# Folds behind the first stage as groups of products on halves of the array's rows, numerators in one piece, and two more steps before the transposes of an x tile

## The chip, the cores and the metric

The kernel runs on one core of one Trainium2 chip. The metric is the device time of one execution in microseconds (us), the median of several runs. The engines are named as the profile names them: PE (TensorE matmul), PEld (its weight load), DVE (VectorE), ACT (ScalarE), POOL (GpSimd) and SP (SyncE, which here issues every transfer between the core's memory and device memory, one after the other).

## The reference

The input x is 2048 x 1024 in float32. Its rows are normalised to xn. Two branches read xn, and the output is their combination:

```python
xn = _layernorm(x, axis=-1)
s = _A_ref(xn, A_wqkv, A_w_phi, A_wo)
g = _silu(_B_ref(xn, B_w_gate, B_w_up, B_w_down))
return x + s * g
```

Branch A is linear attention with 32 heads of width 32 and a learned feature map; branch B is a gated unit of inner width 3584.

```python
qkv = (lambda x, *d: x.transpose(*d))((x @ wqkv).reshape(B, S, 3, H, Dh), 2, 0, 3, 1, 4)
q, k, v = qkv[0], qkv[1], qkv[2]
pq = jnp.einsum("bhsd,hdf->bhsf", q, w_phi)
pk = jnp.einsum("bhsd,hdf->bhsf", k, w_phi)
phi_q = jnp.concatenate([_softmax(pq, axis=-1), _softmax(-pq, axis=-1)], axis=-1)
phi_k = jnp.concatenate([_softmax(pk, axis=-1), _softmax(-pk, axis=-1)], axis=-1)
kv = jnp.einsum("bhsf,bhsd->bhfd", phi_k, v)
num = jnp.einsum("bhqf,bhfd->bhqd", phi_q, kv)
...
# branch B
h = _sigmoid(g) * u
return jnp.einsum("bsf,fd->bsd", h, w_down)
```

Since pq is linear in q, the kernel multiplies w_phi into the q and k columns of wqkv first. That product is what the kernel calls a **fold**.

## The kernel before, in words

All large products are 128 x 128 by 128 x 512. Each operand is kept as a high and a low part, and `mm3` (lines 224 to 226) issues three products for one: high by high, high by low, low by high. Each large matrix product is cut into 2 x 2 blocks and computed with seven block products instead of eight; their names are B11, B21, T2, T3, T4, T1 and B22, in this order. For the projections, one such operation works on four token tiles u = 0..3, whose sums lie in the PSUM banks bank0 to bank3 (98 to 101 in the rows below); an operation is 4 x 4 `mm3`, 48 products. `proj_out` (line 497) takes each of the four sums from its bank behind the operation (`evac`, line 506, on DVE), and some of these results are stored to `qkv_d` at once (line 503). The two buffers for the stored results of T4 are used in turn, so that the third result waits for the first store, and the fourth for the second.

**The first stage** (normalisation, transposes, the first five operations of V for the first half of the tokens, and the folds K 0 to K 2) is written out as a table of steps, FIRST (line 95), and each engine keeps its order. The products stand there as line 996. The table ends with the four takings of T4's sums, in this order: "evac T4 3, ssub t1 1, wsub T1 0, evac T4 1, evac T4 2, evac T4 0".

**Behind it** the order is set by a scheduler, which puts instructions of several traced pieces together by its own estimate of the time; an instruction traced inside `tc.issue_after(i)` is not put ahead of instruction i, and instructions outside it move freely where their operands allow. The operations left of the first token half (V T1, V B22, then seven each for K and Q) are issued in the loop over `ops`; after each token tile's four `mm3`, `step()` takes one entry from the list `side`. The five folds K 3 and Q 0 to Q 3 are entries of that list. `fold(which, k)` loads four raw pieces (`fold_load`, line 323, from `wqkT`), multiplies each by the block-diagonal `bd` in four products of 128 x 128 by 128 columns (`fold_products`, line 329, "a quad" below), copies the results on ACT (`fold_copy`), forms sums on DVE and POOL (`fold_sum`, line 79) and stores seven blocks to `wf_d` (`fold_keep`, line 350), from which the later operations load their weights (line 469). Each record of the profile of such a product in float32 is a half of it, so a quad is 8 records and a fold 32. The raw pieces rotate through four half slots (slots 43 and 54), so a piece of the next fold is loaded when the products on the one before it are done.

**x tiles.** While Q and then the second half's operations run, `paced` spreads background tasks over the products. `x_task` (line 658) loads one tile of the second token half, normalises it, stores it to `xs_d`, loads it back in another arrangement (line 671), yields three times, and then transposes it on DVE (line 672) and forms the operands, with `x_sums` on POOL for every second tile. A yield is the point at which the task gives way until its next turn. The task counts for 8 turns in the pacing.

**The last stage** takes two token tiles at a time (eight pairs). For a pair, seven operations of 4 `mm3` run from the attention output against `wo`. Ahead of them lie the transposes of phi and `numerators` (line 822): 16 products with 64 output rows each (line 832), two of them next to each other in the array's columns, into bank0 to bank3.

The profile's line 220 and 219 are `split` (high part on ACT, low part on DVE), 917 and 920 the same in the first stage, and 1171 and 1188 take sums of the gated unit from their banks.

## Time and profile before

| | |
|---|---|
| time, median of 3 runs | 2351.0 us (2350.98 to 2352.16) |
| the profiled execution | 2350.23 us |
| its span, first to last instruction | 2348.5 us |
| mean granted TensorE clock | 0.999 |
| PE busy | 2331.4 us (99%), 10644 records |
| DVE / ACT / POOL busy | 1624.6 / 957.5 / 1160.7 us |
| transfers | 624.11 MB, mean 266 GB/s |

The profile page lists busy time by engine, the span in 40 slices, the transfer queue, the chain of work that ended last, and the costliest groups of instructions. A row of a group gives line, engine, operation, output and input names, shapes, the count, busy time, the mean of one instruction in ns, and the idle time of its engine just before, with what ended it. A busy PE is not PE at its peak: where products follow each other, the records overlap, so a product's cost is the distance between starts and not its duration.

### The profile page before, as it was taken

The page shows a single profiled execution, that of the slowest core. Times are in us where ns is not written, and L with a number is a line of the kernel's source. Part 1 is how long each engine was busy: PE and PEld are TensorE (multiplying, and loading weights), DVE is VectorE, ACT ScalarE, POOL GpSimd, SP SyncE. Part 2 cuts the span into 40 slices and gives each one's busy share as a digit, 9 for nine tenths or more (in the row PEclk, how much of TensorE's full clock was granted, in tenths as well). Part 3 has the DMA queues.
Part 4 walks back from the last instruction along what each step waited for, and adds up shares of the span by engine and source line. Part 5 has one row for each costly group of instructions (what it writes and reads, how often), then busy time and mean ns, then how long its engine had stood idle before and what let it go on. Part 6 is the DMA issues. An engine that isn't in the chain of part 4 may idle for free.

```text
span 2348.5 us, 32142 instructions
## 1 busy us (share of the span) xinstructions
PE 2331.4 (99%) x10644; PEld 1922.2 (82%) x10644; DVE 1624.6 (69%) x2306; ACT 957.5 (41%) x1410; POOL 1160.7 (49%) x1320
## 2 busy tenths in 40 slices
PE   9999999999999999999999999999999999999999
PEld 7888888878888888888888888888888888887777
DVE  8734788677777675466867777866666777657655
ACT  7333354445454454233435344433434333344322
POOL 3210267677686642304363544555444455623777
PEclk9999999999999999999999999999999999999999
DMA  8875566888888889858888887879777877878774
GB/s 289 298 266 188 188 213 223 278 291 300 304 309 294 281 300 362 303 186 281 270 274 284 281 270 262 287 249 344 245 235 258 276 240 232 285 261 296 241 226 162
DMA packets 265415, 624.11 MB, mean 266 GB/s; under 512 B 36896, under 2 KB 65696, under 8 KB 260640
## 3 DMA queue, kind: packets, MB, share of 16 engines
q1 hardware_dynamic: 265248, 622.05, 78.0%
q8 instruction: 84, 1.38, 0.2%
q14 instruction: 83, 0.68, 0.1%
HBM read 373.42 MB, written 248.51 MB: 265 GB/s over the span
## 4 chain that ended last, share of the span: by engine, by line
PE 90%; DMA 4%; DVE 4%; issue 1%; ACT 1%; POOL 0%; SPq 0%; DVEq 0%; ACTq 0%
PE bank L224 29%; PE bank L225 29%; PE bank L226 29%; DMA fa<-w_down 2%; PE bank L602 1%; PE bank L832 1%; PE bank L329 1%; DMA x<-xk 1%; DVE x L920 1%; DMA fc<-xs_d 0%; DVE x L220 0%; DVE w L220 0%; DMA fa<-wv 0%; DVE w L920 0%; DMA wf_d<-x 0%
## 5 line engine op out<-in xcount | busy, mean ns | idle before, releaser
L225 PE MATMUL bank<-x,w 128*128 128x512 f32 x2352 | 916.4, 390 | 0.7 <-DVE x L220 0.7
L224 PE MATMUL bank<-x,w 128*128 128x512 f32 x2352 | 906.3, 390 | 3.7 <-DVE fc L1171 2.1
L226 PE MATMUL bank<-x,w 128*128 128x512 f32 x2352 | 905.9, 389 | 0.0
L79 POOL TENSOR_TENSOR fc<-fc 128x256 f32<-128x256 f32 x488 | 427.4, 907 | 480.0 <-DMA fc<-e_d 131.6
L220 DVE TENSOR_TENSOR w<-fa,w 128x512 fp32r<-128x512 f32 (+1 forms) x436 | 397.6, 915 | 201.3 <-ACT w L219 191.6
L219 ACT CAST w<-fa 128x512 fp32r<-128x512 f32 (+1 forms) x436 | 300.3, 691 | 556.8 <-PE bank L225 354.5
L224 PEld LDWEIGHTS bank<-x,w 128*128 128x128 f32 x2352 | 441.9, 188 | 97.1 <-DVE fc L1171 2.7
L225 PEld LDWEIGHTS bank<-x,w 128*128 128x128 f32 x2352 | 442.0, 188 | 92.7 <-DVE x L220 1.9
L226 PEld LDWEIGHTS bank<-x,w 128*128 128x128 f32 x2352 | 441.8, 188 | 91.8
L224 PE MATMUL bank<-w,x 128*128 128x512 f32 x636 | 248.4, 391 | 0.3 <-DVE fc L506 0.3
L225 PE MATMUL bank<-w,x 128*128 128x512 f32 x636 | 247.9, 390 | 0.0
L226 PE MATMUL bank<-w,x 128*128 128x512 f32 x636 | 247.4, 389 | 0.0
L79 POOL TENSOR_TENSOR fb<-fa 128x256 f32<-128x256 f32 x112 | 97.9, 894 | 218.6 <-PE bank L226 110.9
L79 POOL TENSOR_TENSOR fb<-fb,fc 128x256 f32<-128x256 f32 x132 | 123.6, 957 | 121.8 <-DVE fc L1188 121.6
L79 POOL TENSOR_TENSOR fc<-fc,sa 128x256 f32<-128x256 f32 x128 | 97.0, 788 | 93.5 <-issue 85.0
L224 PEld LDWEIGHTS bank<-w,x 128*128 128x128 f32 x636 | 119.4, 188 | 26.9 <-issue 1.9
L226 PEld LDWEIGHTS bank<-w,x 128*128 128x128 f32 x636 | 119.4, 188 | 24.8
L225 PEld LDWEIGHTS bank<-w,x 128*128 128x128 f32 x636 | 119.4, 188 | 24.3
L219 ACT CAST p<-fc 128x512 fp32r<-128x512 f32 x96 | 73.0, 764 | 131.2 <-DVE fc L575 79.0
L220 DVE TENSOR_TENSOR x<-fa,x 128x512 fp32r<-128x512 f32 x112 | 93.9, 839 | 45.0 <-ACT x L219 45.0
L219 ACT CAST w<-fb 128x512 fp32r<-128x512 f32 x112 | 69.0, 617 | 118.2 <-PE bank L225 86.4
L1188 DVE TENSOR_TENSOR fc<-fc,bank 128x512 f32<-128x512 f32 x84 | 57.5, 684 | 83.5 <-PE bank L226 61.6
(208 smaller groups left out, 2824.3 us busy)
## 6 DMA issues: line engine op xcount, KB each, us to landing
ws_d<-w SPq DMA_DIRECT2D x112, 512.0 KB, 4.2
w<-ws_d SPq DMA_DIRECT2D x112, 512.0 KB, 5.2
fa<-w_gu SPq DMA_DIRECT2D x84, 512.0 KB, 4.8
fa<-h_d SPq DMA_DIRECT2D x84, 512.0 KB, 4.9
fa<-wf_d SPq DMA_DIRECT2D x32, 1024.0 KB, 6.1
h_d<-fc SPq DMA_DIRECT2D x120, 256.0 KB, 4.7
fa<-w_down SPq DMA_DIRECT2D x80, 256.0 KB, 5.2
h_d<-fb SPq DMA_DIRECT2D x76, 256.0 KB, 4.5
```

The lines of the kernel that those rows point to most:

```text
L79: last = self.engine.tensor_tensor(o[:, s], a[:, s], b[:, s], op=op)
L219: nc.scalar.copy(o[0], src)
L220: return nc.vector.tensor_sub(o[1], src, o[0].bitcast(F32))
L224: nc.tensor.matmul(o, a[0], b[0], start=first, stop=False, **kw)
L225: nc.tensor.matmul(o, a[0], b[1], start=False, stop=False, **kw)
L226: nc.tensor.matmul(o, a[1], b[0], start=False, stop=last, **kw)
L329: nc.tensor.matmul(ps[:, gs], r[:, gs], bd[:, 4 * (n // 2) + g], start=True, stop=True)
L602: nc.tensor.matmul(kvb[g // 2][:, g % 2 * 256:g % 2 * 256 + 256], v[:, g].rearrange("p a f -> p (a f)"), ph[:, g].rearrange("p a f -> p (a ...
L832: nc.tensor.matmul(ps[bs, j * 256:(j + 1) * 256], kv[:, 2 * j + b, bs], ph[:, 2 * j + b], start=True, stop=True, skip_group_check=True)
L920: nc.vector.tensor_sub(o[1], src, o[0].bitcast(F32))
L1188: v = nc.vector.tensor_add(b, u2 if q == 3 else u1, bank)
```

## The change

It has four parts.

1. The five folds behind the first stage are issued by a new function, `fold_group`: 32 products on 64 rows each in place of 16 on 128. `bd` holds 32 x 32 blocks on its diagonal, so the upper 64 rows of a raw piece only reach 64 of the 128 columns and the lower 64 rows the other 64; each half of the rows is multiplied by its 64 columns, and the two halves write two different banks. All 32 stand one after the other, behind the last `mm3` issued (`last_mm`), and the next `mm3` of the projection comes behind them. Four copies on ACT per fold remain, each now of one half of two pieces. Empty entries in `side` put two, one, two, two and two steps ahead of the five folds. The loads for K 3 are issued right behind the first stage, and the loads for the next fold inside each fold, now for Q 0 too.
2. All `mm3` of the projections of the first token half, and those of the last stage, stand behind the one issued before: their order is the order in which they are written, so token tile 0 (bank0) comes first in each operation.
3. The 16 products of `numerators` stand together behind the last `mm3`.
4. `x_task` yields five times ahead of the transposes in place of three, and counts for 10 turns in place of 8.

```diff
--- before.py
+++ after.py
@@ -36,6 +36,9 @@
 
     def next(self):
         self.n += 1
+        return self.now()
+
+    def now(self):
         return self.items[(self.n - 1) % len(self.items)]
 
 
@@ -223,7 +226,7 @@
 
         nc.tensor.matmul(o, a[0], b[0], start=first, stop=False, **kw)
         nc.tensor.matmul(o, a[0], b[1], start=False, stop=False, **kw)
-        nc.tensor.matmul(o, a[1], b[0], start=False, stop=last, **kw)
+        return nc.tensor.matmul(o, a[1], b[0], start=False, stop=last, **kw)
 
     def cut(ab, s):
         return ab[0][:, s], ab[1][:, s]
@@ -316,7 +319,7 @@
     fraw = Ring(halves(43, 11))
     fblock = {K: Ring(((4, 5), (6, 7), (52, 53), (50, 51))), Q: Ring(((52, 53), (50, 51)))}
 
-    folds, folded = {}, {}
+    folds, folded, last_mm = {}, {}, []
 
     def fold_load(which, k, n, r=None):
         r = folds[which, k, n] = fraw.next() if r is None else r
@@ -338,6 +341,38 @@
         else:
             nc.scalar.copy(b, ps)
 
+    def fold_group(which, k):
+
+        with tc.issue_after(last_mm[0]):
+            for n in range(4):
+                if n % 2 == 0:
+                    ps = [tps.next() for _ in range(2)]
+                r = folds.pop((which, k, n))
+                for g in range(4):
+                    for half in range(2):
+                        rs = slice(64 * half, 64 * half + 64)
+                        o = ps[half][:, n % 2 * 256:n % 2 * 256 + 256]
+                        if which == Q:
+                            o = o.rearrange("p (a g d) -> p g a d", a=2, d=DH)[:, g]
+                        else:
+                            o = o.rearrange("p (g f) -> p g f", g=4)[:, g]
+                        m = nc.tensor.matmul(o, r[rs, g * P:(g + 1) * P], bd[rs, 4 * (n // 2) + g, rs], start=True, stop=True,
+                                             skip_group_check=True)
+                if n % 2:
+                    fold_out(which, k, n // 2, ps)
+        last_mm[:] = [m.ins]
+
+    def fold_out(which, k, m, ps):
+        if (which, k) not in folded:
+            folded[which, k] = halves(*fblock[which].now())
+        b = whole(fblock[which].now()[m])
+        for half in range(2):
+            if which == Q:
+                o, l = b.rearrange("p (n g h d) -> p h n g d", n=4, h=2, d=DH)[:, half], ps[half].rearrange("p (n g d) -> p n g d", n=4, d=DH)
+            else:
+                o, l = b.rearrange("p (n h f) -> p h n f", h=2, f=64)[:, half], ps[half].rearrange("p (n f) -> p n f", f=64)
+            nc.scalar.copy(o, l)
+
     def fold_sum(which, k, i, engine):
         a11, a12, a21, a22 = folded[which, k]
         o, a, b, op = ((a22, a21, a22, ALU.add), (a21, a11, a21, ALU.subtract),
@@ -354,12 +389,12 @@
         for n in range(4):
             if (which, k, n) not in folds:
                 fold_load(which, k, n)
-        for n in range(4):
-            fold_copy(which, k, n, fold_products(which, k, n, tps.next()))
+        fblock[which].next()
+        fold_group(which, k)
         fold_keep(which, k, False)
-        if k < 3:
+        if (which, k) != (Q, 3):
             for n in range(4):
-                fold_load(which, k + 1, n)
+                fold_load(*((which, k + 1) if k < 3 else (Q, 0)), n)
         for i in range(4):
             fold_sum(which, k, i, (vector, pool)[i % 2])
         with tc.issue_after(last_sp[0]):
@@ -665,9 +700,8 @@
             nc.sync.dma_start(xs_d[t - CTT, :, :, n].rearrange("q s c -> s q c"),
                               xt[n * DH:(n + 1) * DH].rearrange("s (q c) -> s q c", q=4))
         nc.sync.dma_start(xt, xs_d[t - CTT].rearrange("q s n c -> (q s) (n c)"))
-        yield
-        yield
-        yield
+        for _ in range(5):
+            yield
         for q in range(2):
             nc.vector.transpose(dst[q].rearrange("p (k n s) -> p n k s", n=4, s=DH),
                                 xt.rearrange("p (n k d) -> p n k d", n=4, d=DH)[:, :, 4 * q:4 * q + 4])
@@ -822,16 +856,18 @@
     def numerators(tp_):
 
         sums = []
-        for hb in range(2):
-            for q in range(2):
-                ps, ph = nmr.next(), units_ph[hb, q]
-                kv = slots[KVB[hb]][:, q].rearrange("p (k m) -> p k m", m=P)
-                for j in range(2):
-                    for b in range(2):
-                        bs = slice(b * 64, b * 64 + 64)
-                        nc.tensor.matmul(ps[bs, j * 256:(j + 1) * 256], kv[:, 2 * j + b, bs], ph[:, 2 * j + b], start=True,
-                                         stop=True, skip_group_check=True)
-                sums.append((hb, q, ps))
+        with tc.issue_after(last_mm[0]):
+            for hb in range(2):
+                for q in range(2):
+                    ps, ph = nmr.next(), units_ph[hb, q]
+                    kv = slots[KVB[hb]][:, q].rearrange("p (k m) -> p k m", m=P)
+                    for j in range(2):
+                        for b in range(2):
+                            bs = slice(b * 64, b * 64 + 64)
+                            m = nc.tensor.matmul(ps[bs, j * 256:(j + 1) * 256], kv[:, 2 * j + b, bs], ph[:, 2 * j + b],
+                                                 start=True, stop=True, skip_group_check=True)
+                    sums.append((hb, q, ps))
+        last_mm[:] = [m.ins]
         for hb, q, ps in sums:
             o = oraw[hb].rearrange("p u (g t) -> p u g t", t=P)
             nc.scalar.copy(o[:, :, 2 * q:2 * q + 2], ps.rearrange("p (j u t) -> p u j t", j=2, u=2))
@@ -1044,8 +1080,11 @@
     fraw.items = halves(43, 54)
     while prep():
         pass
-    for w, k in [(K, 3)] + [(Q, k) for k in range(4)]:
+    for w, k, waits in ((K, 3, 2), (Q, 0, 1), (Q, 1, 2), (Q, 2, 2), (Q, 3, 2)):
+        side.extend([lambda: None] * waits)
         side.append(lambda w=w, k=k: fold(w, k))
+    for n in range(4):
+        fold_load(K, 3, n)
 
     gmm = Ring(banks[:4])
     gbank = {}
@@ -1062,7 +1101,7 @@
               ([(t, hb) for t in range(CTT) for hb in range(2)] + [(t, 0) for t in range(CTT, TT)], [(t, 1) for t in range(CTT, TT)])]
     spare = [slots[43][:, 0], slots[43][:, 1], slots[42][:, 0], slots[40][:, 0]]
     wd = [(5, lambda j=j: wd_sums(j, *(halves(47, 52) if j < WD1 else spare))) for j in range(NJ)]
-    xs = [(8, lambda t=t: x_task(t)) for t in (CTT + 4 * a + q for q in range(4) for a in range(2))]
+    xs = [(10, lambda t=t: x_task(t)) for t in (CTT + 4 * a + q for q in range(4) for a in range(2))]
     os = [(6, lambda k=k: o_task(k)) for k in range(4)]
 
     def plain(f, *a):
@@ -1117,8 +1156,13 @@
                 xo = run(XO[i], 4)
                 us = slice(u * P, (u + 1) * P)
                 for k in range(4):
-                    mm3(pbank[u], (xo[:, k, 0, us], xo[:, k, 1, us]), pair(ws[k]),
-                        i in opening and k == 0, k == 3, skip_group_check=True)
+                    with ExitStack() as behind:
+                        if last_mm:
+                            behind.enter_context(tc.issue_after(last_mm[0]))
+                        m = mm3(pbank[u], (xo[:, k, 0, us], xo[:, k, 1, us]), pair(ws[k]),
+                                i in opening and k == 0, k == 3, skip_group_check=True)
+                if c == 0:
+                    last_mm[:] = [m.ins]
                 step()
                 if c and operands.left:
                     operands.step()
@@ -1272,8 +1316,9 @@
         for c in cs:
             for u in range(4):
                 p = 4 * c + u
-                mm3(banks[p], cut(pair(hs[c]), slice(u * P, (u + 1) * P)), pair(w),
+                m = mm3(banks[p], cut(pair(hs[c]), slice(u * P, (u + 1) * P)), pair(w),
                     j == 0 and i in (B11, T2, T3, T1), j == NJ - 1, skip_group_check=True)
+        last_mm[:] = [m.ins]
         wfree.append(w)
         hfree.extend(hs.values())
         if n >= ND - 2 * NJ - 8 and len(WO[B21]) < 4 and hfree:
@@ -1359,7 +1404,9 @@
             ps = abank[{B21: B11, T4: T3, B22: T1}.get(i, i)]
             o = [h.rearrange("p (k t) -> p k t", t=P) for h in pair(of[tp_][i])]
             for k in range(4):
-                mm3(ps, (o[0][:, k], o[1][:, k]), pair(WO[i][k]), i in opening and k == 0, k == 3, skip_group_check=True)
+                with tc.issue_after(last_mm[0]):
+                    m = mm3(ps, (o[0][:, k], o[1][:, k]), pair(WO[i][k]), i in opening and k == 0, k == 3, skip_group_check=True)
+                last_mm[:] = [m.ins]
                 n += 1
                 while nxt and nxt[0][0] <= n:
                     fn, *a = nxt.pop(0)[1]
```

All line numbers behind line 36 move: 224 to 226 become 227 to 229, 323 becomes 326, 350 becomes 385, 506 becomes 541, 832 becomes 867, 996 becomes 1032, and the new products of the folds are line 359.

**PE where V's operation T1 begins.** x_1_611 is the operand of T4, x_1_771 that of T1; bank_98 to bank_101 are bank0 to bank3. Before:

```order
88 L996 MATMUL bank_101<-w_93,x_1_611 128x512 x4
89 L996 MATMUL bank_99<-w_93,x_1_611 128x512 x4
90 L329 MATMUL bank_105<-fb_96,fc_97 128x128
91 L329 MATMUL bank_102<-fb_96 128x128 x4
92 L224 MATMUL bank_101<-w_93,x_1_771 128x512
93 L329 MATMUL bank_104<-fb_96,fc_97 128x128 x4
94 L225 MATMUL bank_101<-w_93,x_1_771 128x512
95 L226 MATMUL bank_101<-w_93,x_1_771 128x512
```

and with the change:

```order
81 L1032 MATMUL bank_101<-w_93,x_1_611 128x512 x6
82 L1032 MATMUL bank_100<-w_93,x_1_611 128x512 x4
83 L1032 MATMUL bank_101<-w_93,x_1_611 128x512 x4
84 L1032 MATMUL bank_99<-w_93,x_1_611 128x512 x4
85 L227 MATMUL bank_98<-w_93,x_1_771 128x512
86 L228 MATMUL bank_98<-w_93,x_1_771 128x512
87 L229 MATMUL bank_98<-w_93,x_1_771 128x512
```

T1 began on bank3 with quads of the fold K 3 around it; now T4 runs through, and T1 begins on bank0, with no fold ahead of it.

**DVE at the same place.** Line 506 (541 with the change) takes a sum from its bank; the rows with x_1_771 and w_93 form low parts. Before:

```order
125 L506 TENSOR_TENSOR fc_97<-fc_97,bank_101 128x512
126 L920 TENSOR_TENSOR x_1_771<-fc_97,x_1_771 128x4x128
127 L920 TENSOR_TENSOR w_93<-p_94,w_93 128x2x512
128 L220 TENSOR_TENSOR w_93<-fa_95,w_93 128x2x512
129 L506 TENSOR_TENSOR fc_97<-fc_97,bank_99 128x512
130 L220 TENSOR_TENSOR w_93<-fa_95,w_93 128x2x512
131 L506 TENSOR_TENSOR fc_97<-fc_97,bank_100 128x512
132 L506 TENSOR_TENSOR fb_96<-fb_96,bank_101 128x512
133 L79 TENSOR_TENSOR fc_97<-fc_97 128x512 x2
134 L506 TENSOR_TENSOR fb_96<-fb_96,bank_99 128x512
135 L506 TENSOR_TENSOR fc_97<-fc_97,bank_98 128x512
```

and with the change:

```order
125 L541 TENSOR_TENSOR fc_97<-fc_97,bank_101 128x512
126 L956 TENSOR_TENSOR x_1_771<-fc_97,x_1_771 128x4x128
127 L956 TENSOR_TENSOR w_93<-p_94,w_93 128x2x512
128 L541 TENSOR_TENSOR fc_97<-fc_97,bank_99 128x512
129 L223 TENSOR_TENSOR w_93<-fa_95,w_93 128x2x512 x2
130 L541 TENSOR_TENSOR fc_97<-fc_97,bank_100 128x512
131 L541 TENSOR_TENSOR fc_97<-fc_97,bank_98 128x512
132 L541 TENSOR_TENSOR fb_96<-fb_96,bank_98 128x512
```

T4's sums are taken in the order bank3, bank1, bank2, bank0 in both. Before, the sums of T1 in bank3 and bank1 (those with fb_96) were taken ahead of T4's in bank0; now bank0's comes fourth, and T1's first sum behind it.

**PE in the last stage**, the numerators of one pair of token tiles (the pairs in the middle are alike). Before, one of their two places is

```order
9486 L226 MATMUL bank_102<-w_93,x_0_91 128x512
9487 L832 MATMUL bank_99<-fb_14626,p_14625 64x256 x3
9488 L832 MATMUL bank_100<-fb_14626,p_14625 64x256 x4
9489 L832 MATMUL bank_101<-fb_14626,p_14625 64x256 x4
9490 L224 MATMUL bank_102<-w_93,x_0_91 128x512
```

(11 products; the other five lie in a place of their own further on). With the change:

```order
9527 L229 MATMUL bank_102<-w_93,x_0_91 128x512
9528 L867 MATMUL bank_98<-fb_14706,p_14705 64x256 x4
9529 L867 MATMUL bank_99<-fb_14706,p_14705 64x256 x4
9530 L867 MATMUL bank_100<-fb_14706,p_14705 64x256 x4
9531 L867 MATMUL bank_101<-fb_14706,p_14705 64x256 x4
9532 L227 MATMUL bank_102<-w_93,x_0_91 128x512
```

All 16 of a pair stand together. Over the stage, the 128 products lay in 18 places and now lie in 10.

## The prediction

> **What bounds the kernel now.** I read the page first.
>
> ```profile
> span 2348.5 us, 32142 instructions
> PE 2331.4 (99%) x10644; PEld 1922.2 (82%) x10644; DVE 1624.6 (69%) x2306; ACT 957.5 (41%) x1410; POOL 1160.7 (49%) x1320
> PE 90%; DMA 4%; DVE 4%; issue 1%; ACT 1%; POOL 0%; SPq 0%; DVEq 0%; ACTq 0%
> ```
>
> TensorE has something to do for 99% of the span, and the chain that ended last runs through it for 90%. So time is won or lost in two ways only: where PE waits, and where its instructions stand further apart than products of one kind do. The second step was the timeline of PE where the first stage ends, and the table by stretches:
>
> ```profile
> 87.81 3.37 PE L996 MATMUL bank<-w,x 128*128 128x512 f32 x14
> 92.63 0.50 PE L224 MATMUL bank<-w,x 128*128 128x512 f32 x1 [0.34 <-DVE fc L506]
> 94.45 1.13 PE L329 MATMUL bank<-fb,fc 128*128 128x128 f32 x8 [1.32 <-DMA fc<-wqkT]
> 95.34 0.47 PE L225 MATMUL bank<-w,x 128*128 128x512 f32 x1
> ...
> 90.50:95.00 4.50, 2.84 (x19) 2.25 (x19) 4.50 (x7) 2.67 (x4) 0.00 (x0) 1.00 0.85 287
> 95.00:106.00 11.00, 11.00 (x65) 9.60 (x64) 6.08 (x10) 1.66 (x3) 2.87 (x4) 1.00 1.02 352
> 495.00:510.00 15.00, 12.88 (x50) 10.16 (x49) 10.53 (x17) 10.30 (x14) 9.72 (x13) 0.89 0.95 318
> ```
>
> A row of the timeline has start, time, instruction, count and the wait ahead of it; a row by stretches has the busy time of PE, PEld, DVE, ACT and POOL, then granted clock and the transfers' share. From 90.5 to 95 DVE is busy throughout (4.50 of 4.50) while PE idles 1.66 us; from 95 to 106 PE has no gap, with quads between the products. A quad of a fold costs 95.34 - 94.45 = 0.89 us (0.111 a record), a fold of four 3.56 us.
>
> **Part 2, the strict order, decides where T1 begins.** T1's first product goes to bank0 now, and must wait until DVE has taken T4's sum out of bank0, the fourth taking. DVE before:
>
> ```profile
> 91.89 0.68 DVE L506 TENSOR_TENSOR fc<-fc,bank 128x512 f32<-128x512 f32 x1
> 92.49 0.69 DVE L920 TENSOR_TENSOR x<-fc,x 128x512 fp32r<-128x512 f32 x1
> 93.09 1.22 DVE L920 TENSOR_TENSOR w<-p,w 128x1024 fp32r<-128x1024 f32 x1
> 94.23 1.22 DVE L220 TENSOR_TENSOR w<-fa,w 128x1024 fp32r<-128x1024 f32 x1
> 95.36 0.68 DVE L506 TENSOR_TENSOR fc<-fc,bank 128x512 f32<-128x512 f32 x1
> 98.68 0.69 DVE L506 TENSOR_TENSOR fc<-fc,bank 128x512 f32<-128x512 f32 x1 [1.50 <-DMA qkv_d<-fc]
> 105.37 0.69 DVE L506 TENSOR_TENSOR fc<-fc,bank 128x512 f32<-128x512 f32 x1 [1.82 <-DMA qkv_d<-fc]
> ...
> 72.01 1.00 SPq L323 DMA_DIRECT2D fb<-wqkT x2
> 73.11 0.89 SPq L350 DMA_DIRECT2D wf_d<-x x2
> ...
> PE bank L329 <- DMA fb<-wqkT: 1.2, 1, 1.2
> ```
>
> Before, T4's sum in bank0 was taken at 105.37, and nobody minded, since T1 began on bank3, freed at 91.89. In the new order the four takings lie closer. The two loads at 72.01 no longer stand ahead of the stores at 73.11, which release the buffers that this chain works in; I let the first taking come 1.1 us earlier, at 90.8. Two starts of 0.60, one of 1.14, and the second taking is at 93.1; 0.60 and two of 1.13 later the third at 96.0, the fourth at 96.6, done at 97.3. PE has finished T4 by about 88.5: 91.0, less the fold's 16 records there (1.8 us) and a wait for a load (1.2), with half a us kept for operands. So it stands some 9 us. Compared at one point of the work: before, at 95.34, the fold K 3 and one product of T1 are done. With the change the same is done at 97.3 + 0.23 + 3.56 + 0.55 (the switch, priced below) = 101.6. This is **+6.3 us**, the K 3 loads' waits of before already taken off. Ends: DVE may be 3 us earlier, if the idle time ahead of the chain goes; or the stores decide, as the third and fourth taking each wait for the store two before. Those took 98.68 - 92.57 = 6.1 and 105.37 - 96.04 = 9.3 us, under a transfer share of 1.02; by them T1 begins at 100.6 to 103.8. I stay near the low end, because PE stands still and the large loads come behind these stores. So +3.3 to +12.8.
>
> A wait also costs clock:
>
> ```profile
> 498.31 0.50 PE L224 MATMUL bank<-x,w 128*128 128x512 f32 x1 [2.12 <-DVE fc L1171]
> 499.31 0.63 PE L224 MATMUL bank<-x,w 128*128 128x512 f32 x1
> 502.29 0.39 PE L225 MATMUL bank<-x,w 128*128 128x512 f32 x1
> ```
>
> After 2.12 us of waiting, seven products from 499.31 take 2.98 us, 0.43 each, against 0.227 elsewhere; eight of them cost **+1.6 us**, and I expect the same behind the longer wait (up to 2.5).
>
> **Part 3, numerators.** Two places in a steady pair of token tiles:
>
> ```profile
> 2216.24 0.39 PE L226 MATMUL bank<-w,x 128*128 128x512 f32 x1
> 2216.55 2.80 PE L832 MATMUL bank<-fb,p 128*64 128x256 f32 x22
> 2219.63 0.40 PE L225 MATMUL bank<-w,x 128*128 128x512 f32 x1
> ...
> 2226.72 0.39 PE L226 MATMUL bank<-x,x 128*128 128x512 f32 x1
> 2227.03 1.51 PE L832 MATMUL bank<-fb,p 128*64 128x256 f32 x10
> 2228.81 0.39 PE L225 MATMUL bank<-x,fa 128*128 128x512 f32 x1
> ```
>
> From the product ahead to the second one behind: 3.39 and 2.09 us. Six pairs of records more cost 1.30, so a pair is 0.217; 3.39 less 11 pairs and two products of 0.227 leaves 0.55 us for entering and leaving the column-tiled mode. The places fall from 18 to 10: 8 x 0.55 = **-4.4 us**. The products stay the same, and their operands are transposed several us ahead, so I add no wait; bounds -5.5 and -2.
>
> **Part 1, the folds.** Five groups enter and leave a tiled mode; if rows cost what columns do, 0.55 each, one of them counted above: **+2.2 us** for the four of Q. Quads cost nothing at their edges before. Inside a group, 32 pairs of records follow each other, two halves side by side. What a pair costs no row shows. The nearest:
>
> ```profile
> L329 PEld LDWEIGHTS bank<-fb x128: 186/192/192, 9.5 to 136.6; 128*128 128x128 f32 x128
> L832 PEld LDWEIGHTS bank<-fb,p x256: 132/137/137, 2129.6 to 2313.6; 128*64 128x64 f32 x128
> 1162.00 1.12 PE L602 MATMUL bank<-p 128*128 128x256 f32 x8
> 1162.96 0.40 PE L224 MATMUL bank<-x,w 128*128 128x512 f32 x1
> ```
>
> Eight products of 256 columns (line 602) take 0.96 us, 0.120 each, more than half of a 512-column product (0.113): the weight load of 128 columns sets the pace. A load of 64 columns is 55 ns shorter than one of 128. So the load goes by columns, and a half of the rows still loads 128: a pair costs 0.11, 32 of them 3.56 us, as before: **0**. Low end: streaming alone, half the columns, 0.056 a pair, -1.8 us a fold, -9 in all. High end: two loads one after the other, 0.22 a pair, +3.6 a fold, +18. I take 0, by the row at 1162.00; the high end is far, since the numerators' two tiles, a pair in 0.217, keep pace side by side.
>
> On this the Trainium skill has two rules. "TensorE: Matmul & The Clock Gate", section "LDWEIGHTS (loading the stationary operand)", gives a load by its columns, not its rows, about 107 ns for 128 columns: by it the groups gain nothing. "TensorEngine Tiling (Array Packing)", section "Theoretical Speedup", promises up to 2x for a contraction of 64: by it the sum would be about 2344, a rival below.
>
> The raw pieces of a fold are loaded into the buffers that the group before has just read. From K 3 to Q 0 a piece has 24 products (5.4), a group (4.1) less a quarter (0.9): 8.6 us; the later ones, behind 36 products (8.2), 11.4.
>
> ```profile
> fc<-wqkT SPq DMA_DIRECT2D x7, 256.0 KB, 7.0
> wf_d<-fc SPq DMA_DIRECT2D x21, 256.0 KB, 6.9
> ```
>
> The medians from 70 to 125 us are 7 us, so the load alone fits. But the last piece for Q 0 stands on SP behind two 1 MB loads from wf_d, of which the first waits for a store to land. I put **+1.0** on it, between 0 and 6. The copies on ACT and the sums hide behind the next operation.
>
> **Part 4, the x tiles.** Around 440 to 510 us:
>
> ```profile
> 446.41 1.30 DVE L672 STREAM_TRANSPOSE fc<-fc 128x512 f32<-128x512 f32 x2 [2.75 <-DMA fc<-xs_d]
> 471.68 1.31 DVE L672 STREAM_TRANSPOSE fc<-fc 128x512 f32<-128x512 f32 x2 [3.67 <-DMA fc<-xs_d]
> POOL fc L79 <- DVE fc L672: 7.1, 1, 7.1
> L224 PE MATMUL bank<-x,w 128*128 128x512 f32 x94 | 37.6, 400 | 3.7 <-DVE fc L1171 2.1 <-DVE fc L1188 1.5
> ```
>
> DVE stands behind a reload that is not there yet, POOL behind DVE for 7.1 us, and PE later for 2.1 and 1.5 on sums that these two deliver; with the half clock at 499 that is 5.2 us. Two tiles lie 25.3 us apart for 8 turns, 3.2 a turn (an estimate), so two turns more cover both waits, and POOL works on other pieces in its 7.1 us. I take **-4.8**; bounds -5.2 and 0, or +2 if the tile's sums come too late.
>
> **Sum** against the profiled execution of 2350.2: 6.3 + 1.6 + 2.2 + 1.0 - 4.4 - 4.8 = +1.9, 2352.1. The median of the runs stands 0.8 above that execution: **2353**.
>
> **Rivals.** (a) The halves run at the streaming pace: 2353 - 9 = 2344. For it: a pair of numerators keeps two tiles busy at once. Against: the row at 1162.00. (b) Slower: SP. If a store's landing (6.9) and a load's (7.0) follow each other on SP's queue for each fold, Q 0 waits 13.9 - 8.6 = 5.3 and the other three 2.5 each: 12.8, 12 more than the sum has, 2365. It decides from 8.6 us on. For it: a share of 1.02 at 95 to 106. Against: while PE stands, the queue empties. (c) The x tiles' waits stay, because POOL is late by its own work: 2358. (d) The two halves load one after the other: 2371. (e) DVE is early and T1 hardly waits, so that the change brings what the numerators and x tiles give: 2347.
>
> **Chances.** My forecast 0.46, its own range 2347 to 2359; (a) 0.15, (b) 0.15, (c) 0.12, (d) 0.05, (e) 0.07. The range 2343 to 2366 leaves out (d), the far end of (a) and (b) with several late loads. A change of 0.2% (4.7 us) is about what can be told from none: below 2346.3 lie most of (a), half of (e) and a part of the forecast, 0.28; above 2355.7 lie (b), (c), (d) and a part of the forecast, 0.37; between, 0.35.
>
> **What would show it.** T1: PE idle for 9 us ahead of line 227, ended by DVE's line 541, then clock below 1. Groups: starts of line 359 pair by pair, 0.11 or 0.056, and 0.55 at the edges. SP: a wait "DMA wqkT" ahead of line 359. Numerators: one place of 32 records a pair, 4.0 us. x tiles: no wait of DVE for xs_d, no PE wait near 485 and 496. Wrong would be: no wait at T1, or groups of 2.4 us or of 7.

## The result: 1.6% slower, all of it before 200 us

Before: 2350.99 us (median of 4 runs, 2349.15 to 2352.16). With the change: **2388.03 us** (4 runs, 2384.92 to 2388.91). The ratio is 1.0157, with a 95% interval of 1.0145 to 1.0169. The prediction, 2353 with a range of 2343 to 2366, was 35 us too low, and its range did not hold the time.

The profiled execution took 2384.92 us. The first rows of its page and the shares of its chain of waits:

```profile
span 2383.1 us, 32452 instructions
PE 2340.1 (98%) x10804; PEld 1929.5 (81%) x10804; DVE 1622.0 (68%) x2306; ACT 957.1 (40%) x1411; POOL 1173.8 (49%) x1320
PE 78%; DMA 5%; DVE 4%; POOL 2%; issue 2%; ACT 1%; SPq 0%; DVEq 0%; ACTq 0%; POOLq 0%
```

Of every engine but PE the busy time is within 1.2% of before. The chain runs through PE for 78% now, and was on it for 90%. The mean granted clock is 0.992, and was 0.999.

Where the time went is read best by setting the k-th product of `mm3` (and of the first stage's table) of the one trace against the k-th of the other; both have 9744 of them, counted from 0. The starts in us, worked out from the two traces:

```
product   before    after    difference
    200    81.22    77.23       -3.99   no fold in the last of V's operations
    240    92.63    96.58       +3.95   T1's first product
    260   101.55   103.00       +1.45   K 3 is still to come after the change
    300   112.42   125.25      +12.83   behind K 3 and Q 0
    340   125.08   144.66      +19.57   behind Q 1
    400   142.28   166.86      +24.57   behind Q 2
    480   162.22   197.84      +35.62   behind Q 3
   1600   423.00   458.77      +35.77
   2000   520.92   551.17      +30.26   behind the x tiles
   8800  2089.59  2122.84      +33.25
   last  2343.36  2377.83      +34.48
```

So some 35.8 us are lost by 200 us, the x tiles give 5.5 back, 3.0 go in small waits between 600 and 900 us, and 1.2 in the last stage. PE's timeline of the stretch in which they are lost, with the change (start, time, instruction, count, wait ahead of it):

```profile
84.84 3.33 PE L1032 MATMUL bank<-w,x 128*128 128x512 f32 x14
96.58 0.77 PE L227 MATMUL bank<-w,x 128*128 128x512 f32 x1 [8.41 <-DVE fc L541]
...
100.13 0.50 PE L229 MATMUL bank<-w,x 128*128 128x512 f32 x1
100.47 0.39 PE L227 MATMUL bank<-w,x 128*128 128x512 f32 x1
...
106.40 0.39 PE L229 MATMUL bank<-w,x 128*128 128x512 f32 x1
106.72 2.00 PE L359 MATMUL bank<-fb 64*128 64x64 f32 x32
108.56 1.95 PE L359 MATMUL bank<-fb,fc 64*128 64x64 f32 x32
110.44 0.50 PE L227 MATMUL bank<-w,x 128*128 128x512 f32 x1
110.78 0.39 PE L228 MATMUL bank<-w,x 128*128 128x512 f32 x1
...
117.94 1.06 PE L359 MATMUL bank<-fb,fc 64*128 64x64 f32 x16
123.34 1.97 PE L359 MATMUL bank<-fb,fc 64*128 64x64 f32 x16 [4.34 <-DMA fc<-wqkT]
...
139.18 3.68 PE L359 MATMUL bank<-fb,fc 64*128 64x64 f32 x32 [2.44 <-DMA fc<-wqkT]
...
148.07 0.42 PE L227 MATMUL bank<-w,x 128*128 128x512 f32 x1
...
156.86 2.34 PE L359 MATMUL bank<-fb,fc 64*128 64x64 f32 x32 [0.95 <-DMA fc<-wqkT]
```

T1 stands 8.41 us, as predicted. The group of K 3 (106.72 to 110.44) runs without a wait: 32 records of a half each, 16 pairs, from 106.72 to 108.56 is 0.115 a pair. But inside the groups of Q 0, Q 1 and Q 2 PE waits for the raw pieces, and behind each of those waits comes a piece of work at half clock: 32 records of Q 1 take 3.68 us where those of K 3 take 1.95. The costliest waits of PE from 70 to 215 us, grouped (total, times, longest), and the table by stretches (busy time of PE, PEld, DVE, ACT, POOL, then clock and transfers' share):

```profile
PE bank L227 <- DVE fc L541: 9.9, 2, 8.4
PE bank L359 <- DMA fc<-wqkT: 7.7, 3, 4.3
PE bank L227 <- ACT fc L547: 5.2, 1, 5.2
...
120.00:140.00 20.00, 14.21 (x92) 12.01 (x94) 4.24 (x6) 5.43 (x9) 2.83 (x4) 0.78 0.71 251
140.00:160.00 20.00, 19.01 (x130) 16.05 (x129) 6.30 (x8) 4.71 (x9) 4.90 (x6) 0.76 0.72 244
```

The sum of all starts that stand too far apart between 76 and 210 us: waits went from 2.9 to 24.3 us, products that follow each other more slowly than at full clock from 1.1 to 13.5, edges of the groups are 1.6. That is 35.4 more; 35.8 were lost. Of the 13.5 us, 12.0 are the clock's: PE is busy for 23.9 us in five stretches with a granted clock of 0.50, where before has 1.00 throughout. The stages' transfers did not become more: their share is 0.71 and 0.72 in the two rows above, and in before 0.98 and 0.88. Before's row for the first of them:

```profile
120.00:140.00 20.00, 20.00 (x118) 17.61 (x117) 5.66 (x7) 8.72 (x13) 2.87 (x4) 1.00 0.98 340
```

The queue has gaps because SP, which issues the transfers in a fixed order, stands. SP with the change (an issue, or a run of them, that takes long is one that waited; line 326 is a raw piece's load, 385 the store of a folded block or a sum, 504 a 1 MB load from wf_d, 538 the store of a projection's sum):

```profile
113.08 0.85 SPq L504 DMA_DIRECT2D fa<-wf_d  x2
114.02 0.38 SPq L326 DMA_DIRECT2D fc<-wqkT  x1
...
124.71 0.32 SPq L385 DMA_DIRECT2D wf_d<-fc  x1
...
125.73 0.40 SPq L326 DMA_DIRECT2D fb<-wqkT  x1
...
131.25 0.88 SPq L326 DMA_DIRECT2D fc<-wqkT  x2
132.19 9.34 SPq L385 DMA_DIRECT2D wf_d<-fc  x2
...
166.48 11.34 SPq L385 DMA_DIRECT2D wf_d<-fc  x5
...
181.52 0.32 SPq L605 DMA_DIRECT2D fc<-qkv_d  x1
```

Q 0's last piece goes out at 114.02, right behind two loads of 1 MB, and its landing lets PE go on at 123.34. Until then Q 0's last blocks can't be copied; their stores stand on SP at 124.71, and Q 1's loads stand behind those, at 125.73 and 131.25. So one late load delays the next fold's loads, and that one's the next. At 166.48 it reaches a load that ACT needs, issued only at 181.52:

```profile
168.87 0.58 ACT L547 COPY fc<-bank 128x512 f32<-128x512 f32 x1 [2.13 <-PE bank L229]
185.76 0.62 ACT L222 CAST p<-fc 128x512 fp32r<-128x512 f32 x1 [16.31 <-DMA fc<-qkv_d]
186.29 2.04 ACT L374 COPY fc<-bank 128x512 f32<-128x512 f32 x4
```

ACT stands 16.31 us for a cast whose operand is not loaded; Q 3's four copies and the taking of a projection's sum (line 547) stand behind it, and PE waits 5.2 us for that taking.

### The profile page after: what moved, and what is told of

Same layout as the page of the kernel before. It is cut to its first block, busy times and chain, and to the rows that moved or that the text cites. A ratio compares the mean times of both kernels' runs of the same rounds, so it can differ in the third digit from the quotient of the medians.

```text
span 2383.1 us, 32452 instructions
## 1 busy us (share of the span) xinstructions
PE 2340.1 (98%) x10804; PEld 1929.5 (81%) x10804; DVE 1622.0 (68%) x2306; ACT 957.1 (40%) x1411; POOL 1173.8 (49%) x1320
## 3 DMA queue, kind: packets, MB, share of 16 engines
q8 instruction: 85, 1.39, 0.2%
## 4 chain that ended last, share of the span: by engine, by line
PE 78%; DMA 5%; DVE 4%; POOL 2%; issue 2%; ACT 1%; SPq 0%; DVEq 0%; ACTq 0%; POOLq 0%
PE bank L227 26%; PE bank L228 25%; PE bank L229 25%; DMA fc<-f_d 2%; POOL fc L82 1%; PE bank L637 1%; DMA fa<-w_down 1%; DVE fb L851 1%; POOL fb L82 1%; DVE x L223 1%; DVE w L223 1%; DMA fc<-xo_d 0%; DMA fc<-x 0%; ACT x L222 0%; PE bank L867 0%
## 5 line engine op out<-in xcount | busy, mean ns | idle before, releaser
L82 POOL TENSOR_TENSOR fc<-fc 128x256 f32<-128x256 f32 x488 | 434.9, 922 | 509.4 <-DMA fc<-e_d 105.5
L223 DVE TENSOR_TENSOR w<-fa,w 128x512 fp32r<-128x512 f32 (+1 forms) x436 | 398.2, 916 | 179.1 <-ACT w L222 161.8
L227 PE MATMUL bank<-w,x 128*128 128x512 f32 x636 | 252.7, 398 | 15.3 <-DVE fc L541 9.9
L228 PE MATMUL bank<-w,x 128*128 128x512 f32 x636 | 251.0, 395 | 0.0
L229 PE MATMUL bank<-w,x 128*128 128x512 f32 x636 | 250.3, 394 | 0.0
L227 PEld LDWEIGHTS bank<-w,x 128*128 128x128 f32 x636 | 121.6, 191 | 44.5 <-issue 10.7
L229 PEld LDWEIGHTS bank<-w,x 128*128 128x128 f32 x636 | 121.4, 191 | 25.9
L228 PEld LDWEIGHTS bank<-w,x 128*128 128x128 f32 x636 | 121.5, 191 | 25.0
L82 POOL TENSOR_TENSOR fb<-fb 128x256 f32<-128x256 f32 x44 | 43.0, 996 | 148.0 <-DMA fb<-w_down 148.0
```

Source lines behind the costliest of these rows:

```text
L82: last = self.engine.tensor_tensor(o[:, s], a[:, s], b[:, s], op=op)
L223: return nc.vector.tensor_sub(o[1], src, o[0].bitcast(F32))
L227: nc.tensor.matmul(o, a[0], b[0], start=first, stop=False, **kw)
L228: nc.tensor.matmul(o, a[0], b[1], start=False, stop=False, **kw)
L229: return nc.tensor.matmul(o, a[1], b[0], start=False, stop=last, **kw)
```

## The experiments

Each time is a median, beside the kernel before on the same chip.

### The parts one by one

**Part 4 alone** on the kernel before: the x tiles' two more steps.

```diff
-        yield
-        yield
-        yield
+        for _ in range(5):
+            yield
...
-    xs = [(8, lambda t=t: x_task(t)) for t in (CTT + 4 * a + q for q in range(4) for a in range(2))]
+    xs = [(10, lambda t=t: x_task(t)) for t in (CTT + 4 * a + q for q in range(4) for a in range(2))]
```

> The kernel before with part 4 alone: five turns ahead of the transposes of an x tile, 10 turns in the pacing. Theory (the gain of 5.1 us between products 1800 and 2000 of the changed kernel is this part's): 2346, no wait of DVE for the reload from xs_d, no wait of PE near 485 and 496. Rival: the waits of 0.5, 0.7 and 1.3 us for ACT's sums near 533, 725 and 840 of the changed kernel come from the longer pacing too; then only 2348.

2348.74 against 2349.78 us, ratio 0.9996 [0.9987, 1.0006]. The two waits at 485 and 496 and the half clock behind them are gone there, but others came. A row of PE's waits in this run, grouped:

```profile
PE bank L224 <- ACT fc L1178: 1.7, 2, 1.1
```

The first of the two is at 691 us, on work that this part doesn't touch, and with shorter waits up to 2012 us they eat what was gained. The local gain is real, and part 4 alone still makes no difference that can be told: the rival's 2348.

**Part 3 alone**: the numerators in one piece, with the strict order of the last stage that the change gives it.

```diff
+        with tc.issue_after(last_mm[0]):
+            for hb in range(2):
...
+        last_mm[:] = [m.ins]
...
-                mm3(ps, (o[0][:, k], o[1][:, k]), pair(WO[i][k]), i in opening and k == 0, k == 3, skip_group_check=True)
+                with tc.issue_after(last_mm[0]):
+                    m = mm3(ps, (o[0][:, k], o[1][:, k]), pair(WO[i][k]), i in opening and k == 0, k == 3, skip_group_check=True)
+                last_mm[:] = [m.ins]
```

> The kernel before with part 3 alone and the strict order of the last stage: numerators in 10 places. Theory (the last stage in strict order waits 1.1 us in each pair for DVE, whose work now comes in one heap): 2352, PE waits for the sums of line 1386 in every pair. Rival (those waits came from elsewhere in the changed kernel): 8 places fewer at 0.55, 2346.6.

2351.89 against 2349.78 us, 1.0009 [0.9999, 1.0018]: no gain. **The same, with the last stage's other products free** to be placed (the wait for last_mm is kept on the numerators alone):

```diff
-                with tc.issue_after(last_mm[0]):
-                    m = mm3(ps, (o[0][:, k], o[1][:, k]), pair(WO[i][k]), i in opening and k == 0, k == 3, skip_group_check=True)
+                m = mm3(ps, (o[0][:, k], o[1][:, k]), pair(WO[i][k]), i in opening and k == 0, k == 3, skip_group_check=True)
                 last_mm[:] = [m.ins]
```

> As part 3 alone, but the products of the last stage may change places again; the 16 numerators of a pair still stand together. If the strict order makes the wait, it goes and 2346.6 is left; if the heap of DVE's work makes it, the time is that of part 3 alone, 2352.

2343.45 against 2349.78 us, **0.9973 [0.9963, 0.9982]**. The costliest of PE's grouped waits in the last stage, first strict, then free:

```profile
PE bank L224 <- DVE fc L1391: 5.0, 5, 1.1
```

```profile
PE bank L225 <- DVE x L220: 1.3, 1, 1.3
```

In the strict order each of five pairs waits 1.1 us for DVE to take a sum of T1 (line 1391) before B22 may begin in its bank; when free, other products stand there. Set product against product with before, the last stage is 0.2 us shorter in the strict run's profile and 6.0 in the free one's. These two profiles lie 9.8 us apart, and the rest of that lies ahead of the last stage (1.6 us by product 260, 2.3 more between 1600 and 2000), where neither edit changes anything. So the fewer places bring somewhat more than was counted, and the order that was to make them takes it back. With part 4 on top:

> The numerators in one piece with a free last stage (2343.5) and the longer x tasks (1 less by themselves), without the folds' change: if they add, 2342.5, the best of the parts. Rival (the later waits for ACT at 690 and 805 grow): 2344 or more.

2343.48 against 2349.52 us, 0.9972 [0.9961, 0.9984]: part 4 adds nothing here either. Part 3 with the last stage free, with or without part 4, is the fastest of all that ran, and beats both kernels.

**Parts 1 and 2 alone**: the groups of halves, spaced, and the strict order of the projections; numerators and x tiles as before.

> Parts 1 and 2 (the groups of folds with their spacing, and the strict order of the first projections), without parts 3 and 4. Theory (all the loss lies ahead of 210 us): 2351 + 39.8 = 2391. Rival (parts 3 and 4 interact with it, as the later waits suggest): 2385 or less.

2387.17 against 2349.78 us, 1.0162 [1.0147, 1.0177]. The time lies between the theory's 2391 and the rival's 2385. The whole loss is here; the runs below start from this kernel, which I call the halves.

### Halves or full rows

The group is kept, at its place and in the strict order, but made of 16 products over all 128 rows (32 records); each piece is copied to its block alone.

```diff
-                    for half in range(2):
-                        rs = slice(64 * half, 64 * half + 64)
...
+                    gs = slice(g * P, (g + 1) * P)
+                    m = nc.tensor.matmul(ps[:, gs], r[:, gs], bd[:, 4 * (n // 2) + g], start=True, stop=True)
-                if n % 2:
-                    fold_out(which, k, n // 2, ps)
+                fold_copy(which, k, n, ps)
```

> As the two parts of the folds alone (2387), but each group has 16 products on all 128 rows in place of 32 on halves; place, spacing, loads and strict order unchanged. Theory (a half of the rows gains nothing: 64 pairs of records at 0.112 are 32 records at 0.112): the same waits, 2 us less for the edges, 2385. Rival (the halves do save time and the waits hide it): slower, 2390.

2361.34 against 2349.29 us, 1.005 [1.0034, 1.0067]: **26 us less than the halves**; neither 2385 nor 2390 was near. Rows of its timeline of PE, of its grouped waits and of its table by stretches:

```profile
107.77 1.95 PE L354 MATMUL bank<-fb 128*128 128x128 f32 x16
109.55 1.95 PE L354 MATMUL bank<-fb,fc 128*128 128x128 f32 x16
```

```profile
PE bank L227 <- DVE fc L534: 8.4, 1, 8.4
...
PE bank L354 <- DMA fc<-wqkT: 1.0, 2, 0.8
```

```profile
120.00:140.00 20.00, 20.00 (x108) 17.25 (x108) 9.95 (x12) 8.01 (x13) 7.64 (x8) 1.00 1.02 362
```

A group's products take what the halves take (107.77 to 109.55 is 1.78 us for half a fold, and 1.84 with the halves). T1 waits the same 8.4 us. What is gone are the waits for raw pieces, but for 1.0 us, and the half clock behind them: PE is busy for 20.00 of 20 us at clock 1.00 where the change has 14.21 at 0.78 (and the run of the halves 14.30 at 0.78), with the transfers' share at 1.02 instead of 0.71. SP in this run:

```profile
111.07 0.89 SPq L326 DMA_DIRECT2D fc<-wqkT  x2
113.15 0.33 SPq L497 DMA_DIRECT2D fa<-wf_d  x1
...
118.08 0.44 SPq L326 DMA_DIRECT2D fb<-wqkT  x1
...
122.41 0.33 SPq L326 DMA_DIRECT2D fc<-wqkT  x1
```

Q 0's last piece goes ahead of the 1 MB loads, and Q 1's loads run from 118.08 to 122.41, where the change has 125.73 to 131.25. Two things differ: the order in which the scheduler laid loads, copies and stores on the engines, and that with halves a block is whole only when two pieces are through the array. To tell them apart, **full rows, but each block filled by two copies of 256 columns** that both wait for a pair of pieces:

```diff
-                fold_copy(which, k, n, ps)
+                if n % 2 == 0:
+                    ps0 = ps
+                    continue
+                for a in range(2):
+                    for b, l in ((folded[which, k][n - 1], ps0), (folded[which, k][n], ps)):
...
+                        nc.scalar.copy(b, l.rearrange("p (g a d) -> p a g d", a=2, d=DH)[:, a])
```

> The groups of 16 full-row products, but every block of a folded piece is filled by two copies of 256 columns that both wait for a pair of pieces, as the halves' copies do; SP's and DVE's orders stay almost those of the full-row groups (16 rows of SP's list differ near its end of the folds, none of DVE's). Theory 1: the order of loads, stores and copies that the halves were given is what costs the 26 us between 2361.3 (full rows) and 2387.2 (halves). Then this run stays near the full rows, 2360 to 2366 (the smaller copies cost ACT some 0.3 us a pair of pieces, off the path). Theory 2: it is that a block can be stored and summed only when two pieces are through the array. Then this run goes most of the way to the halves, 2375 to 2388, with waits ahead of the groups for wqkT of several us in sum (full rows: 1.0).

2361.01 against 2349.56 us, 1.0052 [1.0036, 1.0069]: as fast as full rows. So the need for two pieces costs nothing that can be told. With that and the products' equal time ruled out, the order on the queues is what is left for the 26 us. That is by elimination: halves in the full rows' order on every queue were not run. Nor does any run take apart one more difference between the traces: in the change a wait of 0.95 us inside a group of halves was followed by half clock, and with full rows one of 0.77 us at 156.11 was not. That stretch of half clock cost the change 1.7 us.

### Which part of the order

**The 1 MB loads behind the next fold's loads** on SP:

```diff
-                    nc.sync.dma_start(row4(r), wf_d[what, i])
+                    with ExitStack() as behind:
+                        if last_sp:
+                            behind.enter_context(tc.issue_after(last_sp[0]))
+                        nc.sync.dma_start(row4(r), wf_d[what, i])
```

> As the two parts of the folds alone (2387), with one more order: on SP's queue a 1 MB load from wf_d may not stand ahead of the four loads for the next fold. Theory (with halves the later two of these loads stand behind two loads of 1 MB, with full rows ahead of them; this order alone makes the groups wait): the waits for wqkT of 7.7 us and what follows from them go, 2361 to 2368. Rival (the copies, two for every second piece in place of one for each, make the stores and the loads late): 2380 or more.

2391.26 against 2349.52 us, 1.0173 [1.0155, 1.0191]. Q 0's wait of 4.3 us is gone, and nothing is gained. ACT in this run:

```profile
121.72 2.00 ACT L222 CAST w<-fa 128x1024 fp32r<-128x1024 f32 x2 [9.46 <-DMA fa<-wf_d]
123.62 2.04 ACT L374 COPY fc<-bank 128x512 f32<-128x512 f32 x4
```

The casts of the weights now stand on ACT for 9.46 us until the 1 MB loads land, and Q 0's copies stand behind them. The wait has moved from one queue to the next.

**The stores of a fold's sums behind the next fold's loads**, alone and then with the edit above:

```diff
+        with tc.issue_after(last_sp[0]):
+            while kept:
+                fold_keep(*kept.pop(0), True)
         for i in range(4):
             fold_sum(which, k, i, (vector, pool)[i % 2])
-        with tc.issue_after(last_sp[0]):
-            fold_keep(which, k, True)
+        kept.append((which, k))
...
```

> As the one before, without the rule on the 1 MB loads: only the stores of a fold's sums stand behind the next fold's loads. If each of the two rules removes its own wait, the 4.3 us wait of the first Q fold and its half clock stay (8 in all) and the time lies 8 above the run with both; if the stores alone matter, it is equal to it.

> Halves in groups (2387), with SP's queue put in the order that it has with full rows: the loads for the next fold stand ahead of the 1 MB loads from wf_d and also ahead of the stores of the sums of the fold before. Theory (the 26 us between halves and full rows are SP's order: loads that could go stand behind transfers that wait): near 2361, at most 2368, few waits for wqkT. Rival (the halves themselves cost it, by copies that need two pieces each): 2380 or more.

2379.01 [ratio 1.013, 1.0113 to 1.0147] and 2378.82 us [1.0128, 1.0113 to 1.0143], both against 2348.54. So by the ratios these stores cost some 7.5 us (the intervals with and without just touch), the 1 MB loads nothing net. My expectation for both edits together, 2368 or less if SP's order alone made the loss, is refuted. In the run with both SP still stands from 114.67 to 125.11:

```profile
114.67 0.32 SPq L546 DMA_DIRECT2D qkv_d<-fb  x1
125.11 0.32 SPq L546 DMA_DIRECT2D qkv_d<-fc  x1
```

The store at 125.11 is of a sum that DVE has just taken at 124.40, behind another sum that waited 8.01 us for a store, while ACT stood 9.86 us for the weights' load. A load, ACT's cast, ACT's copies, DVE's sum, the store on SP and the next load hold each other in a ring; to mend one queue's order moves the wait. That is read from the rows of this run; no run broke the ring at every queue.

**More room**: the folds of Q five empty steps apart instead of one or two.

```diff
-    for w, k, waits in ((K, 3, 2), (Q, 0, 1), (Q, 1, 2), (Q, 2, 2), (Q, 3, 2)):
+    for w, k, waits in ((K, 3, 2), (Q, 0, 5), (Q, 1, 5), (Q, 2, 5), (Q, 3, 5)):
```

> As the two parts of the folds alone (2387), but five empty steps in place of one or two ahead of each of the folds Q 0 to Q 3. Theory (a raw piece is asked for only when the group before has read it, and 8 to 11 us are too few for it behind what stands on SP): the 7.7 us of waits for wqkT go, the half clock behind them too (6), and ACT's and DVE's waits at 184 and 196, which follow from them: 2367 to 2373. Rival (SP and ACT stand for stores, and the waits only come later): 2380 or more.

2374.21 against 2349.29 us, 1.0107 [1.0092, 1.0122]: 13 us less than the halves. PE's grouped waits:

```profile
PE bank L227 <- DVE fc L541: 16.2, 3, 8.4
```

No wait for wqkT stands among them, but PE waits three times for DVE's takings, T1's 8.4 us and 7.8 more. Ahead of the second of them DVE stands 16.51 us, until 166.00, for a store of the fold's blocks to land, and the takings stand behind it: I read that as the same ring, entered at another place.

### The strict order at T1

The projections' products are set free, so that T1 may begin in the bank that is free first; on the halves, on the halves five steps apart, and on the full rows.

```diff
-                    with ExitStack() as behind:
-                        if last_mm:
-                            behind.enter_context(tc.issue_after(last_mm[0]))
-                        m = mm3(pbank[u], (xo[:, k, 0, us], xo[:, k, 1, us]), pair(ws[k]),
-                                i in opening and k == 0, k == 3, skip_group_check=True)
+                    m = mm3(pbank[u], (xo[:, k, 0, us], xo[:, k, 1, us]), pair(ws[k]),
+                            i in opening and k == 0, k == 3, skip_group_check=True)
```

> As the two parts of the folds alone (2387), but the projections' products may change places: T1 now begins on bank3 as in the kernel before, the groups stay where they are. Theory (T1's wait for the fourth taking is the strict order's, some 8.4 us of 24 us of waits, and the loads' waits are of their own): T1 begins near 91.5 and the time falls by 4 to 5, 2382. Rival (the loads set the pace, and what T1 no longer waits the groups wait more): 2387.

> Both: products of the projections free to change places, and the folds of Q five steps apart. If T1's wait and the loads' waits are two causes that add, the gains add: 2364 to 2368, and what is left above 2351 is T1's shorter wait with its half clock, the group K 3 that no longer fills it, and the edges of five groups.

> Full rows (2361) and projections whose products may change places. Theory (with the loads in time, T1's shorter wait is a gain): T1 begins near 92, 4 to 5 less, 2356 to 2357. Rival (as with the halves, what T1 gains is waited for later): 2361.

On the halves 2381.18 us, 1.0137 [1.0122, 1.0152], 6 less and near the theory's 2382; with five steps 2381.49 us, 1.0138 [1.0123, 1.0153], where 2364 to 2368 was expected, both against 2349.29; on the full rows 2353.61 against 2349.52 us, 1.0016 [1.0007, 1.0026], below the 2356 expected. PE's timeline of the first:

```profile
90.36 0.47 PE L227 MATMUL bank<-w,x 128*128 128x512 f32 x1 [2.59 <-DVE fc L541]
92.01 0.50 PE L228 MATMUL bank<-w,x 128*128 128x512 f32 x1 [1.17 <-DVE w L955]
...
120.48 1.98 PE L359 MATMUL bank<-fb,fc 64*128 64x64 f32 x16 [6.43 <-DMA fc<-wqkT]
```

T1 waits 3.8 us instead of 8.4, but Q 0 then waits 6.43 instead of 4.3, so a part of what T1 gains is lost again: PE only comes earlier to a raw piece that is not there. Where the loads are in time, with full rows, the same edit brings 7.7 us. With more room between the halves it brings nothing and is 7 us slower than spacing alone.

The ledger of the folds by these runs: halves 2387; with full rows 26 less; with T1 free 8 less; 4 us above before are left. The trace of that last run names about as much: between 76 and 210 us PE waits 5.8 us, and 2.9 in before, and it works 3.0 us at half clock, which costs 1.5; before has none there.

## Why the prediction was wrong, point by point

**T1's wait and its half clock: right.** PE stood 8.41 us, 9 were predicted, and T1 began at 96.58, predicted 97.3. T1's tenth product starts at 100.47, in before at 97.26; with the group of K 3 still to be paid, 3.9 us, that is +7.1 by the place where 6.3 + 1.6 were written down.

**A pair of halves: right.** It was put at 0.11 us, and rows at 106.72 and 108.56 give 0.115, the row's edge included. Neither rival (a), half of that, nor (d), double, took place. The Trainium skill, in "TensorEngine Tiling (Array Packing)", section "Theoretical Speedup", promises up to 2x for a contraction of 64; here halves and full rows take the same 3.6 us a fold, and the measurement decides. **The edges** were put at 0.55 us a group; from 106.40 to 110.78, less two products of 0.227 and 32 pairs of 0.112, they are 0.34.

**The raw pieces: the step that failed.** The prediction put +1.0 on Q 0's last piece, between 0 and 6, and nothing on the others, since "the load alone fits". The late piece behind two 1 MB loads was named, and its wait, 4.3 us, lies within its bounds. But the sum took each fold for itself, from the time its buffer comes free. A load is issued when SP gets to it, and ahead of it stand stores of the fold before, which wait for copies, which wait for that fold's last piece. So one late load became three waits for pieces, 7.7 us in all, and two more, 6.7 us in all, for sums taken late by ACT (5.2) and DVE (1.5). "The copies on ACT and the sums hide behind the next operation" did not hold: SP stands for their stores, and by Q 3 PE itself waits 5.2 us for ACT. Rival (b) had the place, SP, and waits at all four groups, and was given 0.15 and 2365. It sized a wait by the time of one store and one load (13.9 us) and took an empty queue as evidence against it. The empty queue, a share of 0.71, was the sign of SP standing.

**Half clock behind the waits: left out.** Only T1's 1.6 us were in the sum. In all, the clock cost 12.0 us, half as much as all the waits (24.3). Beside the 24.7 us that this place lost over the sum's 11.1, the waits not foreseen (7.7 - 1.0 + 6.7 = 13.4) and the clock (12.0 - 1.6 = 10.4) stand for 23.8.

**Numerators: -4.4 predicted, about +1 found in the change.** Each pair's place is one of 32 records, as said. "I add no wait" failed: the strict order adds one of 1.1 us in each of five pairs. The change's timeline of PE in a steady pair:

```profile
2223.32 0.39 PE L229 MATMUL bank<-w,fa 128*128 128x512 f32 x1
2223.64 3.67 PE L867 MATMUL bank<-fb,p 128*64 128x256 f32 x32
...
2227.58 0.40 PE L228 MATMUL bank<-w,fa 128*128 128x512 f32 x1
...
2236.14 0.50 PE L227 MATMUL bank<-x,x 128*128 128x512 f32 x1 [1.13 <-DVE fc L1433]
```

The wait is not at the numerators, whose operands I looked at, but 12 us behind, where the order forbids what filled it before. With the order free the places' saving is there (-6.3 by the medians). It is more than 4.4, since a place was priced as one thing and is two. From 2223.32 to 2227.58, less 16 pairs of 0.216 and two products of 0.227, entering and leaving cost 0.35 us, not 0.55. The other 0.21 of before is a product without a partner: 14 of its 18 places held an odd number, and the last two records of the 22 start at 2218.76 and 2218.98, one after the other, where records before them start two at a time. By the starts of all places, the sum over them went from 9.4 to 3.6 us.

**x tiles: -4.8 predicted, -5.5 found at their place.** With part 4 alone most of it is lost again further on. PE's grouped waits from 590 to 910 us have this row in the change (as ACT's line 1178, with the same numbers, in the run of part 4 alone), and none before:

```profile
PE bank L227 <- ACT fc L1223: 1.7, 2, 1.1
```

So in a sum over the whole kernel the term should have been near -1, by that run.

**The range.** It was built from cases with one cause each, and (b), at 2365, was the slowest rival inside it. Its price rested on one store and one load. In a ring each delay makes the next and half clock adds to each, so those two rows were no bound: the folds' waits and the clock took 24 us where (b) had 12.

## What to carry to other kernels

When an edit turns interleaved pieces into groups, follow each load of the next group back through the queue that issues it: what stands ahead of it, what that waits for, and whether that leads back to the same group. If it does, price the ring and not the single load, and add the half clock that can follow a wait. A fixed order on a busy engine should be priced by what it forbids, at every place where another product could have filled a wait, and not only at the products it groups.

## What the runs showed of the hardware

- Half clock, from rows of short stretches: in the change the granted clock is 0.50 from 93.5 to 100.3 us, 120.8 to 127.6, 137.9 to 148.1, 158.4 to 161.8 and 185.7 to 192.5, and 1.00 between them. These stretches last 6.8, 6.8, 10.2, 3.4 and 6.8 us, each a whole number of times 3.4. They go with the waits of 8.41, 4.34, 2.44, 0.95 and 5.21 us, the fourth beginning 1.5 us behind its wait; the waits of 1.39 us at 79.69 and 1.53 at 197.84 brought none. The longest was behind a short wait, with the half-row products running in it. The Trainium skill, "TensorE: Matmul & The Clock Gate", section "What's actually happening", has the clock fall after an idle window of about 3.4 us and return after about as much busy time. The lengths agree with such a window, but the fall came after less idle time than a whole one, and in the third stretch PE had to work for 8.9 us, 3.6 of them on half-row products, before the clock returned. What half-row products do to the clock, no run here separates.
- The same work need not meet the same clock: part 4 alone leaves the stage around 95 us as it was, but its profile has a clock of 0.50 from 95.2 to 98.5 us, behind waits of 0.37 and 1.25 us, where before has 1.00 behind waits of 0.34 and 1.32. That alone makes 1.5 us by product 260.
- Records of 64 rows and 64 columns, two halves side by side, take 0.112 us a pair, and one of 128 rows and 128 columns 0.111: cutting a product into halves gains nothing here.
- Entering and leaving a group of halves costs 0.34 us, and a place of column-tiled numerators 0.35. Two column-tiled products side by side take 0.43 us for their two pairs of records, and one without a partner just as long.
